# One common scale for the first weights of an attention and feed-forward kernel, and a constant scale on the sums for h

## The chip, the cores and the metric

The kernel runs on one core of a Trainium2 chip. The metric is device time in microseconds (us), the median of several runs of one program. TensorE is called PE here (PEld is its weight load), VectorE DVE, ScalarE ACT, GpSimdE POOL, and SyncE, which issues all the DMAs, SP.

## The reference

Queries are pooled in pairs, attention follows, and a feed-forward layer whose gate is a cosine:

```python
def _attn_ref(q, k, v):            # 8 batches, 8 heads, 1152 positions, 64 columns
    q_pool = q.reshape(B, H, S // 2, 2, D).mean(axis=3)
    scores = 1.0 / np.sqrt(D) * np.matmul(q_pool, k.transpose(0, 1, 3, 2))
    scores = scores - np.max(scores, axis=-1, keepdims=True)
    attn = np.exp(scores)
    attn = attn / (np.sum(attn, axis=-1, keepdims=True) + 1e-09)
    return np.matmul(attn, v)

def _moe_ref(x, w_in, w_out):      # x: 4608 x 512, w_in: 512 x 2048, w_out: 2048 x 512
    h = x @ w_in
    g = h * np.cos(h)
    return g @ w_out
```

## The kernel before

**Numbers as two halves.** The matrix products need more than one 16-bit float holds. So an operand is scaled by a power of two, rounded to a 16-bit float (the upper half), and what is left over becomes a second 16-bit float (the lower half). A product takes three matmuls: upper by upper, upper by lower, lower by upper. The bound that fixes the power of two is a maximum over the operand.

**Attention.** Two heads make a pair; there are 32 pairs, and each is worked in 10 units (`NU`), nine of them over one block of 128 keys and one (the remainder) for the last 64 queries. A unit's scores go to the one PSUM buffer `st` (L1123; the remainder L1146). ACT reads it with the exponential into `e` or `pp` (L1173). In the first pairs (`NF32`) this stays a 32-bit float and goes as it is into the product with V (L1199, remainder L1248); in later ones ACT casts the upper half (L1179) and POOL or DVE subtracts it for the lower (L1185, L1181). Ahead of a pair, PE works out its scores in tiles `m` (L757, `m0` with its number) and DVE takes their maximum (L771); the maximum is written as a column of the queries' lower half (L983) and so subtracted by the matmul. V's scaling is L1026.

**The first weights.** `w_in` and `w_out` arrive as 64-bit floats, each in 8 pieces of 128 x 1024 numbers. `weight_decode` turns a piece into 32-bit floats with three DVE steps (L516, L519, L522). For the first weights ACT then squares the piece with a running sum as its bound (L529, `AF.Square` with `accum_out`); for the second ones DVE takes the largest magnitude (L533). `weight_scale` takes two pieces: PE spreads both bounds to all partitions (`spread`, L463, tile `wam`), DVE reduces them, makes powers of two in `p2w` and their inverses `wsc` (L543, L431, L439, L547, L548; for the second weights L441 and L425 stand for L431 and L439). `weight_split` scales the piece (ACT, L556), casts the upper half (ACT, L557) and subtracts in four steps for the lower (POOL, L560). `weight_steps` runs as a generator: decode, decode, scale, split, split, and so on. The decoded first pieces lie in the memory that later holds the lower half of the second weights (`w2[1]`), four at a time.

Each two pieces have a scale of their own. So a column table `r1` holds the ratio of the two pieces' scale to the largest one, and `r1a` the same for each block of tokens (L598 to L601, L1338).

**Feed-forward.** A chunk is 256 tokens. `ffn1` (L1459) makes h in PSUM (`f`, two buffers); `evac` reads each tile three times: ACT with the scale `r1` into `hsc` (L1483), ACT with `r1a` rounded to an integer (L1486), DVE the difference from it (L1487). The cosine is a sine table (L1391); DVE multiplies (L1397), ACT casts and POOL subtracts for the halves of g (L1408, L1409). `ffn2` (L1519, the last one L1542) makes the output, which DVE scales (L1563, L1552).

**The order.** The main loop records, for each of the 320 units, scores, preparation of later pairs (`JOBS`), some feed-forward work by a credit (`FRATE`), the value product and one or so step of the weights (`SRATE`: 1.0 a unit until the first weights are ready, then 0.6). The feed-forward waits for the first weights (`w1_ready`) and for the first four pairs. `arrange` then orders each engine's instructions anew: it walks through the recorded nodes with estimated costs, and an engine that is free takes the available node that was recorded earliest. What it finds is fixed with dependencies without semaphores, so on the chip each engine works strictly in that order.

Of the kernel before, what the change touches and what calls it, by code (L numbers as in the profile page):

```python
# [9 lines left out]
F32 = mybir.dt.float32  # L10
# [10 lines left out]
P = 128  # L21
# [327 lines left out]
def tile_attention_ffn(  # L349
# [52 lines left out]
    def constants():  # L402
# [5 lines left out]
            if nf < KT:  # L408
                nc.gpsimd.memset(vc[i][:, :, nf:, D : D + 1], 1.0)

    sizes = (1, NP, B + 2, B + 2, B + 2, NWP)
    small = fix.tile([P, sum(sizes)], F32, name="small")
    ends = [sum(sizes[: i + 1]) for i in range(len(sizes))]
    w1max, p2v, p2b, fsc, osb, r1 = (
        small[:, e - n : e] for n, e in zip(sizes, ends)
    )
    p2w = fix.tile([P, 2, NWP], F32, name="p2w")
    r1a = fix.tile([P, B + 2, NWP], F32, name="r1a")
    left = dram.tile([B * LQ, DM], F32, name="left")

    w1 = [fix.tile([P, HP, DFF], F16, name=f"w1_{i}") for i in range(2)]
# [40 lines left out]
    def spread(dst, mx):  # L462
        nc.tensor.matmul(  # L463
            dst,
            mx.broadcast_to([P, P]),
            ident,
            start=True,
            stop=True,
            skip_group_check=True,
        )  # L470
# [11 lines left out]
    def big_free(n=1):  # L482
        k = len(big_alive)
        return all(x < 0 or not big_alive[x][0] for x in range(k - NBIG, k - NBIG + n))

    def big_take(shape, dtype, name):
        assert big_free()
        alive = [True]
        big_alive.append(alive)
        return sb2.tile(shape, dtype, tag="big", bufs=NBIG, name=name), alive  # L490
# [6 lines left out]
    def weight_load(wi, i):  # L497
        src, rows, width, _ = WDIM[wi]
        raw, alive = big_take([P, rows, width * WORDS], w_in.dtype, "wraw")
        ld = nc.sync.dma_start(raw, src[i].rearrange("p (r w) -> p r w", r=rows))  # L500
        if len(w_loads) > WPRE:
            held(ld, "q2T")
        elif len(w_loads) == WPRE:
            held(ld, "v")
        w_loads.append(ld)
        raws.append((raw, alive))

    def weight_decode(wi, i, ft, mx):
        raw, alive = raws.pop(0)
        if not wide:  # L510
            nc.vector.tensor_copy(ft, raw.rearrange("p r w -> p (r w)"))
        else:
            rv = raw.rearrange("p r (w two) -> p (r w) two", two=2)
            lo32, hi32 = rv[:, :, 0], rv[:, :, 1]
            fu = ft.bitcast(U32)
            nc.vector.tensor_scalar(  # L516
                fu, hi32, 0x07FFFFFF, 3, ALU.bitwise_and, ALU.logical_shift_left
            )
            nc.vector.scalar_tensor_tensor(  # L519
                fu, hi32, 0xC0000000, fu, ALU.bitwise_and, ALU.bitwise_or  # L520
            )
            nc.vector.scalar_tensor_tensor(  # L522
                fu, lo32, 29, fu, ALU.logical_shift_right, ALU.bitwise_or
            )
        alive[0] = False
        _, rows, width, dst = WDIM[wi]
        scratch = dst[0][:, :, i * width : (i + 1) * width]
        if WACT[wi]:
            nc.scalar.activation(  # L529
                scratch, ft.rearrange("p (r w) -> p r w", r=rows), AF.Square, accum_out=mx  # L530
            )
        else:
            nc.vector.tensor_reduce(  # L533
                mx, ft, axis=AX.X, op=ALU.max, apply_absolute_value=True
            )
# [15 lines left out]
    def weight_split(wi, i, ft, sc):  # L551
# [6 lines left out]
        for o in range(0, rows, rows // WCUT):  # L558
            r = slice(o, o + rows // WCUT)
            nc.gpsimd.tensor_sub(lo[:, r], fv[:, r], hi[:, r])  # L560

    def weight_steps():
        stage = w2[1].rearrange("p f e -> p (f e)").bitcast(F32)
        stage = stage.rearrange("p (a w) -> p a w", w=WN)
        todo = [(wi, i) for wi in range(2) for i in range(NWP)]
        while todo:
            (wi, i), todo = todo[0], todo[2:]
            alive = [True]
            if wi == 0:
                fts = [stage[:, i % 4 + a] for a in range(2)]  # L570
            else:
                while not big_free():
                    yield
                ft, alive = big_take([P, 2, WN], F32, "wf")
                fts = [ft[:, a] for a in range(2)]
            mx = sb2.tile([P, 2], BF16, tag="wmx", bufs=1, name="wmx")
            for a in range(2):
                while len(raws) < 2 and loads:
                    while not raws and not big_free():
                        yield  # L580
                    if not big_free():
                        break
                    weight_load(*loads.pop(0))
                if wi == 0 and i + a < 2:
                    yield
                weight_decode(wi, i + a, fts[a], mx[:, a : a + 1])
                while len(raws) < 2 and loads and big_free():
                    weight_load(*loads.pop(0))
                yield
            sc = weight_scale(wi, i, fts, mx)  # L590
            yield
            for a in range(2):
                weight_split(wi, i + a, fts[a], sc[:, a : a + 1])
                yield
            alive[0] = False
            if wi == 0 and i == NWP - 2:
                w1_ready[0] = True
                nc.vector.reduce_max(w1max, p2w[:, 0, :], axis=AX.X)  # L598
                rw = sb2.tile([P, 1], F32, tag="rw", bufs=1, name="rw")
                nc.vector.reciprocal(rw, w1max)  # L600
                nc.vector.tensor_scalar(  # L601
                    r1, p2w[:, 0, :], rw, 2.0 ** (HB - 24), ALU.mult, ALU.mult
                )

    extra = []
    fill = {}
# [725 lines left out]
    def chunk_scales(idx):  # L1332
        pm = pms.pop(idx)
        t = sb2.tile([P, 1], F32, tag="fst", bufs=1, name="fst")
        nc.vector.tensor_mul(t, pm, w1max)
        nc.vector.tensor_scalar_mul(fsc[:, idx : idx + 1], t, 2.0 ** (-4 - HB) / (2.0 * math.pi))
        nc.vector.tensor_scalar_mul(osb[:, idx : idx + 1], t, 2.0 ** (-18 - HB))
        nc.vector.tensor_scalar_mul(r1a[:, idx, :], r1, fsc[:, idx : idx + 1])  # L1338

    def split_x(xp, num, den, nt, xT_out):  # L1340
        ratio = sb2.tile([P, 1], F32, tag="ratio", bufs=1, name="ratio")
# [134 lines left out]
    def evac(ck, g, fp, ps, held):  # L1476
        hsc, y = held[:2]

        def fn():
            wp = (g * GF + fp * 2) // 2  # L1480
            yj = y[:, fp * 2 : fp * 2 + 2]
            ra = r1a[:, ck.idx, wp : wp + 1]
            nc.scalar.activation(  # L1483
                hsc[:, fp * 2 : fp * 2 + 2, :], ps, AF.Copy, scale=r1[:, wp : wp + 1]
            )
            nc.scalar.activation(yj.bitcast(I32), ps, AF.Copy, scale=ra, bias=0.25)  # L1486
            nc.vector.scalar_tensor_tensor(  # L1487
                yj, ps, ra, yj.bitcast(I32), ALU.mult, ALU.subtract
            )
            if fp == GF // 2 - 1:  # L1490
                ew_group(*held, ck.gs)

        return fn
# [305 lines left out]
```

## Time and profile before

| what | value |
|---|---|
| median of 3 runs | 1530.41 us (1527.52 to 1530.5) |
| the profiled execution | 1530.05 us, of which the span of its instructions is 1528.3 us |
| granted TensorE clock, mean over the span | 0.999 |
| first matmul of h (L1459) | 186.0 us after the start |
| first scale step of the first weights, last one (L556) | 45.9 us, 104.4 us |

Times in the profile count from the first instruction. A matmul's own duration is longer than its share of PE, since matmuls overlap; the distance from one start to the next is what it costs. A row of a group of instructions gives line, engine, operation, what is written and read, shapes and count, then the busy time in us, the mean duration in ns, and the idle time of the engine ahead of them with what ended it. Line numbers are those of the kernel before; in the order of the changed kernel the same lines stand up to 20 away (L556 is L555, L557 is L556, L1173 is L1193, L757 is L777, L1199 is L1219, L1146 is L1166).

### The profile page before, as it was taken

What the parts mean: (1) busy time and instruction counts of PE and PEld (TensorE: products, weight loads), DVE (VectorE), ACT (ScalarE), POOL (GpSimd) and SP (SyncE); (2) the same over time, 40 slices, a digit from 0 to 9 for tenths busy, and PEclk for the clock granted to TensorE, in tenths of its full rate; (3) what the DMA queues carried; (4) which work ended last, traced back from release to release, by engine and by line L of the source; (5) the groups of instructions that cost most, each with busy time, mean ns of one, the idle gap of its engine ahead of it and who ended that gap; (6) DMA issues with size and microseconds to landing.
All of it is one profiled execution on the core that took longest, in us unless ns stands there. A gap on an engine that the chain in (4) does not pass through costs nothing.

```text
span 1528.3 us, 39292 instructions
## 1 busy us (share of the span) xinstructions
PE 1492.8 (98%) x16774; PEld 1030.2 (67%) x16774; DVE 1127.6 (74%) x1552; ACT 1172.5 (77%) x1473; POOL 932.3 (61%) x793
## 2 busy tenths in 40 slices
PE   5989999999999999999999999999999999999998
PEld 3767787657666676666667667666666667666665
DVE  7889887787988788977866887888787875343332
ACT  4777679887988788887967887988888787864442
POOL 4654658886676858586565676677767665522222
PEclk9999999999999999999999999999999999999999
DMA  9979633434244454335333235445443321001000
GB/s 268 269 204 197 170 85 69 116 78 112 66 107 101 103 97 97 98 84 125 63 85 73 70 80 118 85 96 111 80 112 90 80 56 31 17 19 32 19 18 21
DMA packets 226047, 145.15 MB, mean 95 GB/s; under 512 B 202384, under 2 KB 204688, under 8 KB 223824
## 3 DMA queue, kind: packets, MB, share of 16 engines
q1 hardware_dynamic: 225872, 142.65, 40.2%
q8 instruction: 131, 2.15, 0.6%
q14 instruction: 44, 0.36, 0.1%
HBM read 74.45 MB, written 10.49 MB: 56 GB/s over the span
## 4 chain that ended last, share of the span: by engine, by line
PE 88%; DVE 6%; ACT 3%; DMA 2%; issue 1%; SPq 0%; POOL 0%; DVEq 0%; ACTq 0%; POOLq 0%
PE f L1459 20%; PE f L1519 20%; PE st L1123 14%; PE ava L1199 9%; PE avb L1199 7%; PE m L757 6%; PE st L1146 2%; PE mx L1519 1%; DVE q1s L706 1%; PE st L1459 1%; DMA kld<-in_k_dram 1%; PE mx L800 1%; PE mx L779 1%; DVE mxs L771 1%; PE avb L1459 1%
## 5 line engine op out<-in xcount | busy, mean ns | idle before, releaser
L1185 POOL TENSOR_TENSOR pp<-e,pp 128x512 f16<-128x512 f32 x374 | 461.8, 1256 | 257.0 <-ACT pp L1179 117.0
L771 DVE TENSOR_REDUCE mxs<-m 128x2 f32<-128x1024 f32 x244 | 297.6, 1220 | 104.0 <-PE m L757 102.6
L1459 PEld LDWEIGHTS <-w 128*128 128x128 f16 x3456 | 331.7, 98 | 59.6 <-issue 1.6
L1459 PE MATMUL f<-xT,w 128*128 128x256 f16 x3048 | 365.8, 273 | 0.0
L1173 ACT ACTIVATE e<-st 128x1024 f32<-128x1024 f32 x267 | 272.5, 1021 | 106.8 <-PE st L1123 84.8
L1519 PE MATMUL f<-w,g 128*128 128x512 f16 x1440 | 332.9, 379 | 0.7 <-DVE y L1487 0.7
L1409 POOL TENSOR_TENSOR g<-hsc,g 128x512 f16<-128x512 f32 x144 | 192.8, 1360 | 162.7 <-ACT g L1408 160.9
L1179 ACT CAST pp<-e 128x1024 f16<-128x1024 f32 x267 | 278.9, 1044 | 10.3 <-PE ava L1199 2.5
L1199 PEld LDWEIGHTS <-pp 128*128 128x128 f16 (+1 forms) x7062 | 240.3, 100 | 62.3 <-issue 14.6
L1519 PEld LDWEIGHTS <-g 128*128 128x128 f16 x1680 | 158.5, 98 | 177.2 <-DVE y L1487 0.9
L1199 PE MATMUL ava<-vc,pp 128*128 128x65 f16 (+5 forms) x4646 | 236.7, 200 | 1.0 <-DVE lx L1313 1.0
L1123 PE MATMUL st<-q1T,k 128*128 128x512 f16 x576 | 219.0, 380 | 4.5 <-ACT pp L1173 4.4
L1123 PE MATMUL st<-q2T,k 128*128 128x512 f16 x576 | 218.8, 380 | 0.0
L1199 PE MATMUL avb<-vc,pp 128*128 128x65 f16 (+1 forms) x3196 | 198.3, 200 | 0.0
L1123 PEld LDWEIGHTS <-k 128*128 128x128 f16 x1152 | 105.3, 99 | 100.0 <-issue 10.8
L1397 DVE TENSOR_TENSOR hsc<-hsc,y 128x512 f32<-128x512 f32 x144 | 135.1, 978 | 26.0 <-ACT y L1391 25.8
L757 PE MATMUL m<-k,q1T 128*128 128x512 f16 x496 | 147.0, 379 | 4.2 <-DVE mxs L771 2.3
L1483 ACT ACTIVATE hsc<-f,small 128x512 f32<-128x512 f32 x127 | 86.6, 682 | 83.9 <-PE f L1459 83.7
L1487 DVE SCALAR_TENSOR_TENSOR y<-f,r1a,y 128x512 f32<-128x512 f32 x127 | 94.6, 745 | 61.1 <-ACT y L1486 56.3
L1181 DVE TENSOR_TENSOR pp<-e,pp 128x1024 f16<-128x1024 f32 x80 | 125.6, 1570 | 17.7 <-ACT pp L1179 17.5
L1408 ACT CAST g<-hsc 128x512 f16<-128x512 f32 x144 | 83.3, 613 | 11.6 <-PE f L1519 11.6
L1486 ACT ACTIVATE y<-f,r1a 128x512 int32<-128x512 f32 x127 | 86.2, 679 | 0.0
(180 smaller groups left out, 1786.2 us busy)
## 6 DMA issues: line engine op xcount, KB each, us to landing
vld<-in_v_dram SPq DMA_DIRECT2D x32, 576.0 KB, 3.9
kld<-in_k_dram SPq DMA_DIRECT2D x30, 576.0 KB, 4.2
qld<-in_q_dram SPq DMA_DIRECT2D x30, 576.0 KB, 4.4
k<-k SPq DMA_DIRECT2D x31, 288.0 KB, 3.6
wraw<-in_moe_w_in_dram SPq DMA_DIRECT2D x8, 1024.0 KB, 9.0
wraw<-in_moe_w_out_dram SPq DMA_DIRECT2D x8, 1024.0 KB, 5.9
out_dram<-ob SPq DMA_DIRECT2D x32, 256.0 KB, 2.4
left<-lx SPq DMA_DIRECT2D x64, 16.0 KB, 2.0
```

The costliest lines, as they stand in the source:

```text
L757: nc.tensor.matmul(banks[h], q1T[n][:, h * QT + t, :], kmain(n, k1[n % 3], c, h), start=True, stop=True, skip_group_check=True,),
L771: nc.vector.reduce_max(mxs[n][:, t : t + QT + 1 : QT, c], m, axis=AX.X)
L1123: nc.tensor.matmul(s[:, y, :].rearrange("p (t c) -> p t c", c=P), kcol(p, w, j, h), x[:, h * QT : (h + 1) * QT, :], start=part == 0, stop= ...
L1173: nc.scalar.activation(e, s, AF.Exp, scale=exp_scale, bias=l_add)
L1179: nc.scalar.copy(pp[:, 0, c0:n], e[:, c0:n])
L1181: nc.vector.tensor_sub(pp[:, 1, c0:n], e[:, c0:n], pp[:, 0, c0:n])
L1185: nc.gpsimd.tensor_sub(pp[:, 1, c], e[:, c], pp[:, 0, c])
L1199: mm = nc.tensor.matmul(out, w, x, start=start, stop=False, skip_group_check=True)
L1397: nc.vector.tensor_mul(hj, hj, y[:, j : j + 2])
L1409: nc.gpsimd.tensor_sub(gt[:, 1], hj, gt[:, 0])
L1459: mm = nc.tensor.matmul(ps[:, fi, :], w1[wt][:, hp, fs], ck.xT[hp][:, xi, cs], start=n == 0, stop=n == 3 * HP - 1, skip_group_check=True,)
L1519: nc.tensor.matmul(po, gt[:, gi, f % 2, ts_], w2[wt][:, f, :], start=f == 0 and (gi, wt) == (0, 0), stop=f == NF - 1 and (gi, wt) == (1, 0),)
```

## The change

A new generator `first_weights` takes the place of `weight_steps` for the first weights. It decodes all eight pieces, four into `w2[1]` and four into `w2[0]`, each with its square sum into one column of a tile `mx`; reduces the eight to one, spreads it with one matmul, and makes one bound `w1max` and one inverse `sc`; then splits all eight pieces with `sc`. `weight_steps` goes on with the second weights as before. The tables `r1` and `r1a` go: h leaves PSUM with the constant 2^(HB - 24), and the two other reads take the block's column `fsc`.

```diff
+    def first_weights():
+        stage = [
+            w.rearrange("p f e -> p (f e)").bitcast(F32).rearrange("p (a w) -> p a w", w=WN)
+            for w in (w2[1], w2[0])
+        ]
+        fts = [stage[i // 4][:, i % 4] for i in range(NWP)]
+        mx = sb2.tile([P, NWP], BF16, tag="wmx1", bufs=1, name="wmx1")
+        for i in range(NWP):
...
+            weight_decode(0, i, fts[i], mx[:, i : i + 1])
...
+            yield
+        one = sb2.tile([P, 1], BF16, tag="wmx2", bufs=1, name="wmx2")
+        nc.vector.reduce_max(one, mx, axis=AX.X)
+        am = psum.tile([P, P], F32, tag="f", bufs=2, name="wam")
+        spread(am, one)
+        mw = sb2.tile([P, 1], F32, tag="rw", bufs=1, name="rw")
+        nc.vector.reduce_max(mw, am, axis=AX.X)
+        all_max_end(w1max, mw, WACT[0])
+        sc = sb2.tile([P, 1], F32, tag="wsc1", bufs=1, name="wsc1")
+        nc.vector.reciprocal(sc, w1max)
+        nc.vector.tensor_scalar_mul(sc, sc, 2.0**14)
+        yield
+        for i in range(NWP):
+            weight_split(0, i, fts[i], sc)
+            yield
+        w1_ready[0] = True
+
     def weight_steps():
...
-        todo = [(wi, i) for wi in range(2) for i in range(NWP)]
+        yield from first_weights()
+        todo = [(1, i) for i in range(NWP)]
...
-            if wi == 0 and i == NWP - 2:
-                w1_ready[0] = True
-                nc.vector.reduce_max(w1max, p2w[:, 0, :], axis=AX.X)
-                rw = sb2.tile([P, 1], F32, tag="rw", bufs=1, name="rw")
-                nc.vector.reciprocal(rw, w1max)
-                nc.vector.tensor_scalar(
-                    r1, p2w[:, 0, :], rw, 2.0 ** (HB - 24), ALU.mult, ALU.mult
-                )
...
-        nc.vector.tensor_scalar_mul(fsc[:, idx : idx + 1], t, 2.0 ** (-4 - HB) / (2.0 * math.pi))
+        nc.vector.tensor_scalar_mul(fsc[:, idx : idx + 1], t, 2.0**-28 / (2.0 * math.pi))
...
-        nc.vector.tensor_scalar_mul(r1a[:, idx, :], r1, fsc[:, idx : idx + 1])
...
-            ra = r1a[:, ck.idx, wp : wp + 1]
+            ra = fsc[:, ck.idx : ck.idx + 1]
             nc.scalar.activation(
-                hsc[:, fp * 2 : fp * 2 + 2, :], ps, AF.Copy, scale=r1[:, wp : wp + 1]
+                hsc[:, fp * 2 : fp * 2 + 2, :], ps, AF.Copy, scale=2.0 ** (HB - 24)
             )
```

More of the change, by code (lines that the diff above doesn't have):

```diff
@@ L409, in constants @@
                 nc.gpsimd.memset(vc[i][:, :, nf:, D : D + 1], 1.0)
-    sizes = (1, NP, B + 2, B + 2, B + 2, NWP)
+    sizes = (1, NP, B + 2, B + 2, B + 2)
     small = fix.tile([P, sum(sizes)], F32, name="small")
     ends = [sum(sizes[: i + 1]) for i in range(len(sizes))]
-    w1max, p2v, p2b, fsc, osb, r1 = (
+    w1max, p2v, p2b, fsc, osb = (
         small[:, e - n : e] for n, e in zip(sizes, ends)
@@ L417, in tile_attention_ffn @@
     p2w = fix.tile([P, 2, NWP], F32, name="p2w")
-    r1a = fix.tile([P, B + 2, NWP], F32, name="r1a")
     left = dram.tile([B * LQ, DM], F32, name="left")
@@ L560, in weight_split @@
             nc.gpsimd.tensor_sub(lo[:, r], fv[:, r], hi[:, r])
+    def first_weights():
[6 more added lines that the diff above has]
+        for i in range(NWP):
+            while len(raws) < 2 and loads:
+                while not raws and not big_free():
+                    yield
+                if not big_free():
+                    break
+                weight_load(*loads.pop(0))
+            if i < 2:
+                yield
+            weight_decode(0, i, fts[i], mx[:, i : i + 1])
+            while len(raws) < 2 and loads and big_free():
+                weight_load(*loads.pop(0))
+            yield
[9 more added lines that the diff above has]
+        nc.vector.tensor_scalar_mul(sc, sc, 2.0**14)
+        yield
+        for i in range(NWP):
+            weight_split(0, i, fts[i], sc)
+            yield
+        w1_ready[0] = True
@@ L562, in weight_steps @@
     def weight_steps():
-        stage = w2[1].rearrange("p f e -> p (f e)").bitcast(F32)
-        stage = stage.rearrange("p (a w) -> p a w", w=WN)
-        todo = [(wi, i) for wi in range(2) for i in range(NWP)]
+        yield from first_weights()
+        todo = [(1, i) for i in range(NWP)]
         while todo:
             (wi, i), todo = todo[0], todo[2:]
[L568 to L575, printed above, removed]
+            while not big_free():
+                yield
+            ft, alive = big_take([P, 2, WN], F32, "wf")
+            fts = [ft[:, a] for a in range(2)]
@@ L583, in weight_steps @@
                     weight_load(*loads.pop(0))
-                if wi == 0 and i + a < 2:
-                    yield
                 weight_decode(wi, i + a, fts[a], mx[:, a : a + 1])
@@ L1479, in fn @@
         def fn():
-            wp = (g * GF + fp * 2) // 2
             yj = y[:, fp * 2 : fp * 2 + 2]
-            ra = r1a[:, ck.idx, wp : wp + 1]
+            ra = fsc[:, ck.idx : ck.idx + 1]
             nc.scalar.activation(
-                hsc[:, fp * 2 : fp * 2 + 2, :], ps, AF.Copy, scale=r1[:, wp : wp + 1]
+                hsc[:, fp * 2 : fp * 2 + 2, :], ps, AF.Copy, scale=2.0 ** (HB - 24)
             )
```

## The prediction

> **What bounds the kernel now.** I read the page first: engine shares, then the chain.
>
> ```profile
> span 1528.3 us, 39292 instructions
> PE 1492.8 (98%) x16774; PEld 1030.2 (67%) x16774; DVE 1127.6 (74%) x1552; ACT 1172.5 (77%) x1473; POOL 932.3 (61%) x793
> PE 88%; DVE 6%; ACT 3%; DMA 2%; issue 1%; SPq 0%; POOL 0%; DVEq 0%; ACTq 0%; POOLq 0%
> ```
>
> TensorE is busy in 98% of the span and makes 88% of the chain. Its work hardly changes here, so the question is how much TensorE stands still, before and after. Second view: busy times by stretch (start:end, length, then busy time and count of PE, PEld, DVE, ACT, POOL, the granted clock, DMA).
>
> ```profile
> 40.00:90.00 50.00, 47.66 (x466) 37.59 (x465) 45.07 (x72) 40.49 (x52) 29.15 (x27) 1.00 1.05 271
> 90.00:110.00 20.00, 16.29 (x169) 11.99 (x168) 18.72 (x29) 15.19 (x21) 10.93 (x14) 1.00 0.69 207
> 110.00:165.00 55.00, 53.78 (x487) 43.17 (x487) 50.51 (x80) 36.73 (x50) 28.96 (x30) 1.00 0.81 187
> 165.00:180.00 15.00, 12.98 (x135) 8.71 (x134) 11.47 (x20) 10.26 (x14) 8.87 (x9) 0.89 0.54 140
> 200.00:1528.00 1328.00, 1317.72 (x15143) 896.41 (x15142) 953.74 (x1293) 1037.00 (x1294) 823.78 (x673) 1.00 0.34 77
> ```
>
> PE stands still for 2.3, 3.7, 1.2 and 2.0 us in the first four stretches, and for 10.3 us in the 1328 us after 200. All the first-weight work lies before 110 us, in attention alone, where DVE is busy for 18.7 of 20 us. Idle time there can't be caught up later, since nothing later has slack on PE: each microsecond won or lost counts once in the total.
>
> What stops PE there I read in ACT's row of instructions (third view, the timeline: start, duration, operation, in brackets the idle time before it). L1173 is the exponential of one attention unit. The scores have one PSUM buffer (`st`), so PE can't write the next unit's scores until this one's exponential is done.
>
> ```profile
> 82.79 1.02 ACT L1173 ACTIVATE pp<-st 128x1024 f32<-128x1024 f32 x1 [1.55 <-PE st L1123]
> 83.71 1.14 ACT L556 ACTIVATE w<-w,wsc 128x1024 f32<-128x1024 f32 x1
> 84.75 0.23 ACT L983 ACTIVATE qs<-m 128x9 f16<-128x9 f32 x1
> 84.88 1.05 ACT L557 CAST w<-w 128x1024 f16<-128x1024 f32 x1
> 85.83 1.25 ACT L1026 ACTIVATE vc<-vld,sv 128x1152 f32<-128x1152 f32 x1
> 86.99 1.13 ACT L556 ACTIVATE w<-w,wsc 128x1024 f32<-128x1024 f32 x1
> 88.03 1.00 ACT L1173 ACTIVATE pp<-st 128x1024 f32<-128x1024 f32 x1
> ...
> 98.96 1.04 ACT L529 ACTIVATE w<-w 128x1024 f16<-128x1024 f32 x1
> 99.91 0.19 ACT L529 ACTIVATION_READ_ACCUMULATOR w<-w 128x1 bf16 x1
> ...
> 100.19 1.00 ACT L1173 ACTIVATE pp<-st 128x1024 f32<-128x1024 f32 x1
> ...
> 102.27 1.15 ACT L556 ACTIVATE w<-w,wsc 128x1024 f32<-128x1024 f32 x1 [0.91 <-DVE wsc L548]
> 103.45 1.04 ACT L557 CAST w<-w 128x1024 f16<-128x1024 f32 x1
> 104.40 1.15 ACT L556 ACTIVATE w<-w,wsc 128x1024 f32<-128x1024 f32 x1
> ...
> 107.01 1.02 ACT L1173 ACTIVATE pp<-st 128x1024 f32<-128x1024 f32 x1
> ```
>
> Weight work between two exponentials parts them by 5.2 us (82.79 to 88.03) and by 6.8 us (100.19 to 107.01). The first lies in a stretch where PE hardly stops, the second in the one that loses 3.7 us. So other work for PE covers a parting of some 5 us; beyond that PE waits.
>
> **The change part by part.** *The hole in the exponentials.* The scale of any piece is now known only after all eight, so all sixteen ACT steps of the splits (scale, L556, now L555; cast, L557, now L556) come free at once, and the planner takes what was recorded earlier. This is ACT's row, first before (around the third pair of pieces; `w` is the weight, `pp<-st` the exponential), then now.
>
> ```order
> L1173 ACTIVATE pp<-st 128x1024 x2
> L556 ACTIVATE w_1_84<-w_1_84,wsc 128x1024
> L983 ACTIVATE qs_71<-m 128x9
> L557 CAST w_0_81<-w_1_84 128x4x256
> L1026 ACTIVATE vc_75<-vld,sv 128x18x64
> L556 ACTIVATE w_1_84<-w_1_84,wsc 128x1024
> L1173 ACTIVATE pp<-st 128x1024
> L557 CAST w_0_81<-w_1_84 128x4x256
> L1173 ACTIVATE pp<-st 128x1024 x2
> ```
>
> ```order
> L555 ACTIVATE w_1_83<-w_1_83,wsc_742 128x1024
> L556 CAST w_0_80<-w_1_83 128x4x256
> L555 ACTIVATE w_1_83<-w_1_83,wsc_742 128x1024
> L1003 ACTIVATE qs_71<-m 128x9
> L555 ACTIVATE w_1_83<-w_1_83,wsc_742 128x1024 x2
> L556 CAST w_0_80<-w_1_83 128x4x256
> L555 ACTIVATE w_0_82<-w_0_82,wsc_742 128x1024
> L1046 ACTIVATE vc_75<-vld,sv 128x18x64
> L555 ACTIVATE w_0_82<-w_0_82,wsc_742 128x1024
> L556 CAST w_0_80<-w_1_83 128x4x256
> L555 ACTIVATE w_0_82<-w_0_82,wsc_742 128x1024 x2
> L1193 ACTIVATE pp<-st 128x1024
> ```
>
> Two scale steps at most stood between exponentials; now eight, three casts, the maximum's write (L1003) and a V scaling (L1046) stand in one row, with an exponential ahead and one behind. Their price, start to start in the rows above: a scale step followed by its own cast 1.18 (102.27 to 103.45), the seven others 1.04 each (86.99 to 88.03), casts 0.95 each (103.45 to 104.40), L1003 0.13, L1046 1.16: 1.18 + 7.28 + 2.85 + 0.13 + 1.16 = 12.6 us. The first waits for the scale: from the last piece's square to the first scale step 98.96 to 102.27 = 3.3 us. So from the square to the end of the next exponential pass 3.3 + 12.6 + 1.0 = 16.9 us, 16.8 of them after the previous exponential. What PE has meanwhile stands in its row (around unit 19; `m0` the score tiles for the maxima, `st_1007` the scores that wait for that exponential):
>
> ```order
> L1219 MATMUL avb_817<-vc_1_76,pp_980 128x65 x4
> ...
> L777 MATMUL m0_933<-k1_0_91,q1T_798 128x512
> ...
> L777 MATMUL m0_962<-k1_0_91,q1T_798 128x512
> ...
> L777 MATMUL m0_987<-k1_0_91,q1T_798 128x512
> ...
> L777 MATMUL m0_1040<-k1_0_91,q1T_798 128x512
> L1166 LDWEIGHTS k1_2_93
> L1166 MATMUL st_1007<-q1T_393,k1_2_93 128x64
> ```
>
> ```order
> L757 MATMUL m0_943<-k1_0_92,q1T_803 128x512
> L1199 MATMUL ava_768<-vc_1_76,pp_991 128x65 x4
> L1199 MATMUL avb_822<-vc_1_76,pp_991 128x65 x4
> ...
> L757 MATMUL m0_972<-k1_0_92,q1T_803 128x512
> ...
> L1146 MATMUL st_1018<-q1T_394,k1_2_94 128x64
> ```
>
> The upper row is now, the lower before: one `m0` tile stood between the last attention-value work and the next scores; now four do. They fill part of the hole. Prices from PE's timeline:
>
> ```profile
> 84.43 0.59 PE L757 MATMUL m<-k,q1T 128*128 128x512 f16 x2
> 84.86 0.38 PE L1123 MATMUL st<-q1T,k 128*128 128x512 f16 x1
> ...
> 85.72 1.00 PE L1199 MATMUL avb<-vc,pp 128*128 128x65 f32 x8
> 86.56 1.06 PE L1199 MATMUL ava<-vc,pp 128*128 128x65 f32 x8
> ```
>
> Start to start: an `m0` tile 0.43, a unit's scores 0.86, a group of four value matmuls 0.84. From the scores before the hole to `st_1007` PE has two scores (1.72), six `m0` tiles (2.58), five value groups (4.2) and small ones, which I put at 0.35: 8.85 us in 16.8. **PE idles about 8.0 us.** The bounds: 16.8 if PE had no work there; 5 if PE enters 3 us behind ACT, about one unit.
>
> *The clock.* The row 165:180 has a granted clock of 0.89. By pieces (columns as above):
>
> ```profile
> 172.00:174.00 2.00, 2.00 (x17) 1.72 (x16) 1.97 (x3) 0.00 (x0) 0.26 (x1) 0.81 0.25 52
> 174.00:176.00 2.00, 2.00 (x14) 1.06 (x14) 1.27 (x6) 0.53 (x1) 0.00 (x0) 0.50 1.11 171
> 176.00:178.00 2.00, 2.00 (x24) 0.88 (x21) 1.12 (x1) 1.97 (x3) 0.35 (x1) 0.83 0.72 188
> ```
>
> After a stretch in which PE idled 2 us in all, its clock fell to half: 2 x (0.19 + 0.50 + 0.17) = 1.7 us of work lost. The hole is emptier, so I add 1.7 (0 to 3.4). The Trainium skill ("TensorE: Matmul & The Clock Gate", section "HAM oscillation") sets the danger at idle gaps over about 3.4 us. By that rule the `m0` tiles, which cut the hole into shorter gaps, would keep the clock up and the sum would be 1.7 lower. The trace disagrees: no gap in these rows was that long, and the clock fell, so the row decides.
>
> *Stalls that go.* The partings of before that cost 3.7 us in 90:110 lose their weight work. The hole's leftovers (five casts, a K cast) still stand among the exponentials behind it, so I credit half, -1.9 (0 to -3.7).
>
> *DVE.* The scale group per pair of pieces is one group for all. Its rows, from DVE's groups between 40 and 106 us:
>
> ```profile
> L771 DVE TENSOR_REDUCE mxs<-m 128x2 f32<-128x1024 f32 x18 | 21.9, 1219 | 3.5 <-PE m L757 3.4
> ...
> L543 DVE TENSOR_REDUCE wmw<-wam 128x2 f32<-128x256 f32 x4 | 1.7, 417 | 0.3 <-PE wam L463 0.3
> ...
> L431 DVE TENSOR_SCALAR wmw<-wmw 128x2 uint32<-128x2 uint32 x4 | 1.1, 282 | 0.1
> ...
> L439 DVE TENSOR_SCALAR p2w<-wmw 128x2 f32<-128x2 f32 x4 | 0.7, 170 | 0.1
> L548 DVE TENSOR_SCALAR wsc<-wsc 128x2 f32<-128x2 f32 x4 | 0.7, 169 | 0.1
> L547 DVE RECIPROCAL wsc<-p2w 128x2 f32<-128x2 f32 x4 | 0.7, 166 | 0.2
> ```
>
> 417 + 282 + 170 + 169 + 166 = 1.2 us; three groups fewer is 3.6 us of DVE. PE's idle time before the hole is only the 2.3 of 40:90, so I take -1 (0 to -3.6). Seven broadcast matmuls of 128 columns fewer (`wam`), at the `m0` tile's 0.43 for 1024 columns, are 0.05 each, -0.4.
>
> *The reads of h.* ACT's copy of the sum gets a constant for a column, and the column table r1a goes.
>
> ```profile
> L1483 ACT ACTIVATE hsc<-f,small 128x512 f32<-128x512 f32 x127 | 86.6, 682 | 83.9 <-PE f L1459 83.7
> ...
> L1173 ACT ACTIVATE pps<-f 128x128 f32<-128x128 f32 x3 | 0.8, 271 | 0.0
> ...
> L1338 DVE TENSOR_SCALAR r1a<-small 128x8 f32<-128x8 f32 x10 | 4.6, 464 | 0.0
> ...
> PE f L1519 <- DVE y L1487: 0.7, 2, 0.4
> ```
>
> Exponentials, with constant scale and bias, take 271 ns for 128 columns and 1.02 us for 1024; between them 512 columns cost 0.59, so each copy may save 0.09 us, 13 us of ACT over 144. ACT is 77% busy, and of PE's waits the last row is all that its list lays to these reads: 0.7 us (waiter, releaser, sum, times, longest). I count 0, and +-3 for the new order over the 1328 us with their 10.3 us of PE idle.
>
> *Sum.* +8.0 + 1.7 - 1.9 - 1 - 0.4 = +6.4 us. The profiled execution took 1530.05 us (span 1528.3), 0.4 below the median of 1530.41, so 1530.05 + 6.4 = **1536.4 us**. A measurement of this kernel can tell about 0.2%, 3 us.
>
> **The rivals.** *DVE sets the pace and the hole is free: no change.* In the new order DVE has, between the scale and the reduction that follows `st_1007`, six `m0` reductions of 1.22 us and 3.5 us of other steps, 10.8 of 13.6 us. If DVE is the bound of this stage, the hole costs 13.6 - 10.8 = 2.8 and the clock 1.7, against 3.6 + 0.4 + some stalls: 1530 us. For it: DVE's 18.7 of 20 us in 90:110. Against: over 110:165 DVE works 50.5 of 55 us and PE 53.8, so PE is the tighter one. It decides where the four `m0` tiles leave PE no stall in units 20 to 24. Chance 0.23.
>
> *Faster: the lighter reads count.* If ACT's 13 us and DVE's 4.6 us of r1a halve PE's 10.3 us after 200, 5 us go, and with the hole free as above: 1525 us. Against it is the 0.7 us in the list of waits. It needs both, so 0.14.
>
> *The hole is heavier.* No stall goes, the clock falls twice (3.4), and the lower halves on POOL, eight pieces in one row now, hold back what attention needs by half the hole again: 8.0 + 3.4 + 4 = 15.4, 1545 us. For it: POOL's subtractions can no longer be spread. Against: POOL is busy for 10.9 of 20 us. Chance 0.13. The forecast keeps 0.50.
>
> **How the numbers follow.** The forecast's own range is 1533.5 to 1541. Slower takes forecast and heavier hole, 0.63; within 0.2% 0.23; faster 0.14. For 8 in 10 the range goes from 1527, leaving out the faster end, to 1545.
>
> **What would show it.** Right: in the changed profile two exponentials near 85 to 105 us are 14 to 16 us apart with a row of L555 between, PE idles about 8 us there in pieces ended by `m` reductions and an exponential, and a half clock follows; after 200 us PE's idle time stays near 10 us; the copy of h falls from 682 towards 590 ns with no effect. Wrong: the exponentials stay under 8 us apart, or PE's idle time before 200 us is not larger than before, or the difference arises after 200 us.

## The result, and the profile after

| what | before | after |
|---|---|---|
| median | 1530.41 us (5 runs, 1527.52 to 1531.61) | 1537.04 us (5 runs, 1536.22 to 1543.44) |
| ratio | | 1.0059, 95% interval 1.0044 to 1.0074 |
| the profiled execution | 1530.05 us, span 1528.3 | 1543.44 us, span 1541.7 |

The change costs 6.6 us, 0.6%, against a forecast of +6.4. The profiled execution of after is the slowest of its five, 6.4 us above their median, so its rows show where time goes and only roughly how much. Totals and chain of after:

```profile
span 1541.7 us, 39270 instructions
PE 1499.8 (97%) x16767; PEld 1032.2 (67%) x16767; DVE 1101.1 (71%) x1525; ACT 1162.1 (75%) x1473; POOL 913.4 (59%) x793
PE 85%; DVE 4%; ACT 4%; DMA 3%; issue 2%; SPq 0%; POOL 0%; ACTq 0%; DVEq 0%; POOLq 0%
```

DVE works 26.5 us less and ACT 10.4 us less than before (1127.6 and 1172.5), and the kernel is slower: neither sets the end. PE's busy time grew by 7 us although it has seven matmuls fewer, since a matmul at half clock counts as busy for longer (a pair of matmuls on `m` 1.01 us instead of 0.59, in the rows of the first place below). By stretches (start:end, length, busy time and count of PE, PEld, DVE, ACT, POOL, the granted clock, DMA):

```profile
40.00:90.00 50.00, 48.57 (x469) 37.65 (x468) 43.07 (x63) 32.59 (x46) 9.25 (x8) 1.00 0.94 262
90.00:110.00 20.00, 14.51 (x92) 9.98 (x92) 13.71 (x18) 16.78 (x20) 17.14 (x21) 0.66 0.77 241
165.00:200.00 35.00, 29.11 (x283) 21.13 (x281) 28.56 (x43) 22.10 (x28) 20.81 (x23) 0.85 0.54 119
200.00:1300.00 1100.00, 1094.08 (x13344) 744.49 (x13342) 857.34 (x1173) 909.46 (x1129) 742.07 (x614) 1.00 0.40 90
```

In 90:110 PE starts 92 matmuls where it started 169, is idle for 5.5 us, and runs at a clock of 0.66. In 165:200 it is idle for 5.9 us. From 200 to 1300 PE is busy for 1094.1 us, before for 1093.4: the loss is not there. The same row of before for the third stretch:

```profile
165.00:200.00 35.00, 32.98 (x346) 24.85 (x345) 31.29 (x41) 24.46 (x31) 22.08 (x23) 0.95 0.55 133
```

So there are two places, and the second, 3.9 us more idle time at 165 to 200 us, stands nowhere in the prediction.

**The first place.** ACT's row of after (start, duration, operation, in brackets the idle time before it):

```profile
84.87 1.05 ACT L528 ACTIVATE w<-w 128x1024 f16<-128x1024 f32 x1
85.81 0.20 ACT L528 ACTIVATION_READ_ACCUMULATOR w<-w 128x1 bf16 x1
86.54 1.02 ACT L1193 ACTIVATE pp<-st 128x1024 f32<-128x1024 f32 x1 [0.53 <-PE wam L462]
87.63 1.15 ACT L555 ACTIVATE w<-w,wsc 128x1024 f32<-128x1024 f32 x1
...
98.10 2.19 ACT L555 ACTIVATE w<-w,wsc 128x1024 f32<-128x1024 f32 x2
100.19 1.00 ACT L1193 ACTIVATE pp<-st 128x1024 f32<-128x1024 f32 x1
```

The two exponentials are 13.65 us apart, and the row of splits between them takes 12.56 us (87.63 to 100.19). PE's row of the same time:

```profile
85.42 0.38 PE L1143 MATMUL st<-q1T,k 128*128 128x512 f16 x1
...
88.72 0.38 PE L1143 MATMUL st<-q1T,k 128*128 128x512 f16 x1
...
94.50 0.59 PE L777 MATMUL m<-k,q1T 128*128 128x512 f16 x2 [1.32 <-DVE mxs L791]
96.41 0.92 PE L777 MATMUL m<-k,q1T 128*128 128x512 f16 x2 [1.32 <-DVE mxs L791]
...
98.65 1.01 PE L777 MATMUL m<-k,q1T 128*128 128x512 f16 x2 [1.10 <-DVE mxs L791]
101.24 0.21 PE L1166 MATMUL st<-q1T,k 128*128 128x64 f16 x1 [1.58 <-ACT pp L1193]
```

As forecast, three gaps are ended by reductions of `m` and the fourth by the exponential. The `m` tiles of 96.41 and 98.65 last longer than the one of 94.50 (0.92 and 1.01 against 0.59): the clock has fallen. By pieces (columns as above):

```profile
94.00:96.00 2.00, 0.59 (x2) 0.19 (x2) 1.32 (x2) 2.00 (x3) 1.90 (x4) 1.00 0.84 157
96.00:98.00 2.00, 1.13 (x6) 0.55 (x6) 1.83 (x3) 2.00 (x3) 2.00 (x3) 0.64 0.36 37
101.00:106.00 5.00, 4.76 (x46) 4.39 (x45) 4.09 (x6) 3.35 (x5) 4.85 (x6) 0.50 0.67 259
106.00:110.00 4.00, 3.83 (x12) 1.95 (x13) 1.32 (x5) 2.43 (x4) 2.96 (x5) 0.50 0.85 322
```

The half clock stays until 110 us, for 9 us after PE has all its work again.

**The second place.** ACT's rows of after, and behind them PE's:

```profile
174.13 1.15 ACT L707 CAST kst<-kld 128x1152 f16<-128x1152 f32 x1 [1.40 <-issue]
175.19 1.02 ACT L1193 ACTIVATE e<-st 128x1024 f32<-128x1024 f32 x1
```

```profile
172.78 0.38 PE L1143 MATMUL st<-q1T,k 128*128 128x512 f16 x1 [0.96 <-ACT pp L1193]
176.26 0.59 PE L1143 MATMUL st<-q1T,k 128*128 128x512 f16 x1 [2.34 <-ACT e L1193]
...
181.03 1.01 PE L777 MATMUL m<-k,q1T 128*128 128x512 f16 x2 [1.32 <-DVE mxs L791]
```

PE waits for exponentials that ACT does late, and has little else: the cast of K (L707), ahead of which ACT stood idle for 1.40 us, comes before the exponential in ACT's row. The clock falls here too in this execution (0.85 in 165:200, and the pair of matmuls on `m` at 181.03 lasts 1.01 us).

To see where the order gives PE how much, I laid PE's matmuls in the trace against the order one by one, cut them into attention units (from a unit's first score matmul to the next unit's), and took each unit's work as its matmuls at the median start-to-start distance of their line and shape. What a unit lasts beyond its work I call its excess. Units 41, 42 and 43 hold 3.3, 2.9 and 3.1 us of work before, and 1.3, 1.0 and 7.0 us after: the value work and a score tile that kept PE busy between exponentials now stand behind the scores of unit 43.

The excess in us, by ranges of units, from one profile each (the runs from e1_spread on are told below; e4_warm and e10_ahead_warm count their idle matmuls as work):

```
run              0-17  18-23  24-39  40-45  46-99  100-318   sum   profiled us
before            3.3    4.5   -0.5    3.9   -1.2     0.9   10.9     1530.05
after             4.7   11.0   -0.6    9.4   -1.6     2.2   25.0     1543.44
e1_spread         3.2    3.6    1.2    6.7   -2.0     2.5   15.2     1531.78
e2_reads          3.1    5.0   -0.6    2.8   -2.1    -0.5    7.8     1527.76
e3_weights        2.8   10.7   -0.7    6.3   -1.4     1.7   19.4     1535.64
e4_warm           2.8    2.5   -0.7    7.4   -2.0     2.4   12.2     1533.88
e5_delay          3.8    2.6   -0.2    2.0    5.2    -0.9   12.4     1529.89
e6_delay_alone    3.6    8.4    6.2    0.9    5.2    -0.5   23.8     1541.46
e7_ahead          4.3    7.4   -0.4    1.4   -0.9     2.2   14.0     1532.92
e8_both           4.6    1.4   -0.1    2.0    5.2    -0.5   12.7     1530.03
e9_six            3.8    1.4    0.4    3.2    6.1     3.5   18.4     1533.69
e10_ahead_warm    6.3    0.5    0.2    2.2    4.6     1.3   15.1     1538.11
e11_columns       4.2    1.4    0.0    2.9    0.7     0.5    9.8     1528.28
e12_shift         2.6    4.4    0.7    2.3    1.9     1.2   13.0     1530.78
```

A line's time less its sum lies between 1515.3 and 1520.0 us, but for the two with idle matmuls (1521.7 and 1523.0). What the sum leaves out thus differs by up to 4.7 us from run to run, so the table is used for places, and times are compared by medians. Of after's 9.4 us in units 40 to 45 some belong to the half clock of its execution: the profile of e3_weights, the same first weights, has a full clock there and 6.3 us.

### The profile page after: what moved, and what is told of

Same layout as the page of the kernel before. It is cut to its first block, busy times and chain, and to the rows that moved or that the text cites. A ratio compares the mean times of both kernels' runs of the same rounds, so it can differ in the third digit from the quotient of the medians.

```text
span 1541.7 us, 39270 instructions
## 1 busy us (share of the span) xinstructions
PE 1499.8 (97%) x16767; PEld 1032.2 (67%) x16767; DVE 1101.1 (71%) x1525; ACT 1162.1 (75%) x1473; POOL 913.4 (59%) x793
## 4 chain that ended last, share of the span: by engine, by line
PE 85%; DVE 4%; ACT 4%; DMA 3%; issue 2%; SPq 0%; POOL 0%; ACTq 0%; DVEq 0%; POOLq 0%
PE f L1478 19%; PE f L1537 19%; PE st L1143 14%; PE ava L1219 9%; PE avb L1219 7%; PE m L777 6%; PE st L1166 2%; PE mx L1537 1%; DMA vld<-in_v_dram 1%; DVE mxs L791 1%; DMA wraw<-in_moe_w_in_dram 1%; PE mx L799 1%; PE mx L820 1%; PE st L1478 1%; ACT e L1193 1%
## 5 line engine op out<-in xcount | busy, mean ns | idle before, releaser
L777 PE MATMUL m<-k,q1T 128*128 128x512 f16 x496 | 150.4, 387 | 9.9 <-DVE mxs L791 7.8
L1505 DVE SCALAR_TENSOR_TENSOR y<-f,small,y 128x512 f32<-128x512 f32 x127 | 94.6, 746 | 73.0 <-ACT y L1504 72.6
L1501 ACT ACTIVATE hsc<-f 128x512 f32<-128x512 f32 x127 | 75.1, 592 | 91.0 <-PE f L1478 91.0
L708 POOL TENSOR_TENSOR kst<-kld,kst 128x1152 f16<-128x1152 f32 x30 | 72.8, 2428 | 33.2 <-ACT kst L707 33.0
```

The source lines that it names most:

```text
L777: nc.tensor.matmul(banks[h], q1T[n][:, h * QT + t, :], kmain(n, k1[n % 3], c, h), start=True, stop=True, skip_group_check=True,),
```

## The experiments

Theory at the start: the eight splits in one row make the hole, and the hole with its half clock is the whole loss. Rivals: the loss is in the second place or after it, or in the reads.

**e1_spread: the row taken apart.** The changed kernel, with the scale step of piece n kept behind the exponential of unit 18 + n by an added dependency for the planner.

```diff
+SPREAD0 = 18
...
-        nc.scalar.activation(ft, ft, AF.Copy, scale=sc)
+        first = nc.scalar.activation(ft, ft, AF.Copy, scale=sc)
+        if wi == 0:
+            w1_scales.append(first)
...
+    for n, x in enumerate(w1_scales):
+        after(x, exps[SPREAD0 + n])
     arrange(tc, nc, extra, fill)
```

> The changed kernel, with one thing added: in the planner the scale step of piece n may not stand ahead of the exponential of unit 18 + n, so that one scale step and one cast at most stand between two exponentials. Nothing of the computation changes. Theory (the row of eight scale steps makes a hole of 13.65 us between two exponentials, PE idles in it and then runs at half clock): the longest parting of exponentials between 80 and 130 us falls under 7 us, the half clock near 100 us goes, and the median falls by 5 to 9 us, to 1528 to 1532. Rival (the 6.6 us come from elsewhere, from the new order of the later stages or from the later start of the feed-forward): 1535 or more.

Measured: 1534.05 us (6 runs, 1531.78 to 1535.31), ratio to before 1.0032 (1.0019 to 1.0045). Its stretches (columns as above):

```profile
90.00:110.00 20.00, 16.98 (x174) 12.70 (x173) 18.86 (x23) 16.08 (x21) 14.93 (x18) 1.00 0.79 219
165.00:200.00 35.00, 29.52 (x308) 21.93 (x308) 30.58 (x48) 22.96 (x30) 23.00 (x21) 1.00 0.41 106
```

The hole and its half clock are gone (174 matmuls and clock 1.00 in 90:110, better than before's 16.29 us), but only 3 of the 6.6 us went with them, which is between the theory's range and the rival's. (The longest parting of exponentials is 7.21 us, 89.16 to 96.37, where under 7 was expected; ACT itself is idle for 3.15 us of it.) The second row is poor here too (PE busy for 29.52 us, before for 32.98), without any half clock: the second place doesn't follow from the hole. The theory of one place fell. The 3 us aren't the hole's whole price either: by the table 7.4 us go in units 18 to 23, and 1.8 come back in units 24 to 39.

**e2_reads: the constant reads alone.** The kernel before, with the change's constant scale for h and the block's column for the other two reads; the ratio of the pieces' scales is left out.

```diff
...
-            ra = r1a[:, ck.idx, wp : wp + 1]
+            ra = fsc[:, ck.idx : ck.idx + 1]
             nc.scalar.activation(
-                hsc[:, fp * 2 : fp * 2 + 2, :], ps, AF.Copy, scale=r1[:, wp : wp + 1]
+                hsc[:, fp * 2 : fp * 2 + 2, :], ps, AF.Copy, scale=2.0 ** (HB - 24)
             )
```

> The kernel before with the second part of the change alone: h leaves PSUM with the constant scale and the two other reads take the block's column; the first weights keep a scale for each two pieces. The ratio of a piece's scale to the largest one is left out. Theory (this part costs nothing and gains nothing, since ACT is not what PE waits for): 1527 to 1533.5, the same as before within 3 us, although the copy of h falls from 682 to about 590 ns. Rival (the reads are where the loss or a gain lies): outside of that.

Measured: 1526.75 us (12 runs, 1525.08 to 1528.66), 0.9984 (0.9975 to 0.9994): 2.5 us faster than before in the same session (1529.26), 0.25 us under the expected range and so on the rival's side, and the fastest kernel of the study. **e3_weights** is the counterpart: the new first weights, with column reads (the table filled for eight equal scales).

> The changed kernel with the first part alone: one common scale for the first weights as changed, but h leaves PSUM with a column table as before (the table now holds the same constant eight times). Theory: the hole is as in the changed kernel, 1535 to 1540, with the copy of h at 682 ns. Rival (the loss lies in the constant reads, or in both together): below 1533.

Measured: 1537.17 us (6 runs, 1535.64 to 1540.2), 1.0055 (1.0042 to 1.0069). The copy of h, first in after, then in e3_weights (groups of ACT: busy time, mean ns of one, idle time before):

```profile
L1501 ACT ACTIVATE hsc<-f 128x512 f32<-128x512 f32 x127 | 75.1, 592 | 91.0 <-PE f L1478 91.0
```

```profile
L1507 ACT ACTIVATE hsc<-f,small 128x512 f32<-128x512 f32 x127 | 86.6, 682 | 75.2 <-PE f L1483 75.1
```

The constant saves 90 ns a copy, ACT then waits longer for PE, and the two kernels differ by 0.13 us. The loss belongs to the first weights and the order that comes with them, not to the reads. What the reads had gained in the kernel before wasn't explained yet.

**e4_warm: the half clock by itself.** The changed kernel, with 90 idle matmuls of 128 columns for PE in the hole, whose results nothing reads.

```diff
+WARM = (91.7, 90, 0.1)
...
+        for n in range(WARM[1]):
+            mm = nc.tensor.matmul(
+                big_am[:, P : 2 * P], ident, ident, start=True, stop=True, skip_group_check=True
+            )
+            fill[mm.ins.name] = WARM[0] + WARM[2] * n
```

> The changed kernel with 90 idle matmuls of 128 columns on PE inside the hole, 5 us of PE work that nothing reads, between the m tiles. The hole itself stays. Theory (of the 6.6 us the hole's idle time is the larger part, and the half clock after it, 13.65 us long in the profiled execution, adds 3 to 5 us): the clock stays full between 90 and 115 us and the median falls by 2 to 5 us, to 1532 to 1535. Rival (the half clock costs nothing, since the exponentials set the pace there anyway): no change, 1536 to 1540, though the clock is full. A second rival (the matmuls delay what PE has to do): over 1540.

Measured: 1533.69 us (9 runs, 1532.01 to 1534.78), 1.0031 (1.0021 to 1.0041), 3.35 us under after, inside the expected range. The clock stays full (columns as above):

```profile
90.00:110.00 20.00, 17.60 (x230) 13.87 (x229) 18.23 (x22) 17.29 (x21) 18.33 (x18) 1.00 0.73 228
```

PE's rows: the scores ahead of the hole, those that end it, and the first scores of unit 24, in e4_warm and then, for the last, in after.

```profile
86.10 0.38 PE L1150 MATMUL st<-q1T,k 128*128 128x512 f16 x1
...
98.62 0.19 PE L1173 MATMUL st<-q1T,k 128*128 128x64 f16 x1 [0.58 <-ACT pp L1200]
...
109.61 0.38 PE L1150 MATMUL st<-q1T,k 128*128 128x512 f16 x1
```

```profile
115.65 0.38 PE L1143 MATMUL st<-q1T,k 128*128 128x512 f16 x1
```

The hole is the same length: 86.10 to 98.62 is 12.52 us, and 88.72 to 101.24 in after is 12.52 too. Behind it PE needs 10.99 us to unit 24 with the idle matmuls and 14.41 us without. So the half clock costs nothing in the hole and 3.4 us behind it.

**e5_delay and e6_delay_alone: the second place.** The planner takes steps in the order in which the units record them, one weight step a unit. The old first weights had 22 such steps (2 and 4 times 5), the new ones have 19 (2 + 8 + 1 + 8), so every step of the second weights is recorded three units earlier, at another point of the attention pairs' rhythm. e6_delay_alone adds three empty steps to the changed kernel, e5_delay to e1_spread:

```diff
+        for _ in range(3):
+            yield
         w1_ready[0] = True
```

> The changed kernel with the scale steps spread as in the first experiment (1534.05 us there), and with three empty steps added at the end of the first weights, so that the steps of the second weights are recorded in the same units as before the change (the change leaves 19 steps where there were 22, so they came three units earlier). The planner then puts the last 128 columns of that pair's scores, and the bound of m after it, back into units 41 and 42, where only about 1.0 to 1.3 us of PE work a unit was left. Theory (the rest of the loss is this second place, PE's excess over its work in units 40 to 46 being 6.7 us against 3.9 before): 1530.5 us, 1528.5 to 1532, and that excess 3 to 4.5 us. Rival (the rest comes from elsewhere, such as longer work on DVE or the smaller stalls at 110 to 140 us): it stays at 1533 to 1535 us whatever the excess in those units does.

Measured: 1531.49 us (12 runs, 1529.6 to 1534.81), 1.0015 (1.0006 to 1.0024), 2.6 us under e1_spread, with an excess in units 40 to 45 of 2.0 us, less than the 3 to 4.5 expected. Its row of the second place:

```profile
165.00:200.00 35.00, 33.46 (x370) 26.35 (x368) 31.82 (x47) 24.22 (x31) 23.79 (x22) 1.00 0.58 133
```

PE starts 370 matmuls where e1_spread started 308. The theory of the second place holds. But in units 46 to 99 the excess is 5.2 us, where the kernels so far have -1.2 to -2.1: the new order had a stall of its own there, so the 2.6 us are what is left after it.

> The changed kernel with the three empty steps alone; the scale steps stay in one row, so the hole near 100 us and its half clock stay. Theory of two separate places: 1533 us, 1531.5 to 1535, with PE's excess in units 18 to 24 still 10 to 11 us and in units 40 to 46 3 to 4.5 us. Rival (the second place only follows from the hole, as lateness handed on): the empty steps alone change nothing and it stays at 1536 to 1538 us.

Measured: 1541.46 us (5 runs, 1538.68 to 1543.6), 1.0079 (1.0066 to 1.0092). Both expectations missed. The hole stayed (excess 8.4 in units 18 to 23), the second place closed (0.9), and a third opened, in units 33 and 34. POOL's, DVE's and PE's rows there:

```profile
137.85 2.40 POOL L710 TENSOR_TENSOR kst<-kld,kst 128x1152 f16<-128x1152 f32 x1
```

```profile
138.06 3.26 DVE L521 SCALAR_TENSOR_TENSOR wf<-wraw,wf 128x1024 uint32<-128x1024 uint32 x1
141.25 1.21 DVE L793 TENSOR_REDUCE mxs<-m 128x2 f32<-128x1024 f32 x1
```

```profile
142.51 0.59 PE L779 MATMUL m<-k,q1T 128*128 128x512 f16 x2 [1.94 <-DVE mxs L793]
```

A decode step of DVE, 1.22 us in the median of its group, took 3.26 us beside a subtraction on POOL; the reduction behind it came late; PE stood still for 1.94 us, and the clock fell:

```profile
143.00:148.00 5.00, 5.00 (x29) 4.16 (x28) 3.71 (x7) 0.29 (x1) 0.74 (x2) 0.56 0.85 203
148.00:154.00 6.00, 6.00 (x25) 4.17 (x25) 1.31 (x3) 1.02 (x1) 0.00 (x0) 0.51 0.78 218
```

**e7_ahead: a smaller dose of the hole.** The three empty steps ahead of the eight splits instead of behind them, in the changed kernel.

> The changed kernel with the three empty steps ahead of the eight splits instead of behind them. The second weights come as in the experiment before; and of the eight scale steps five instead of eight stand between the same two exponentials. Theory (the hole's price goes with the number of scale steps in one row, about 1.15 us for each): the two exponentials are 9.5 to 10.5 us apart instead of 13.65, PE's excess in units 18 to 24 falls to 6 to 8 us from 11, and the time is 1531 us, 1528.5 to 1533. Rival (the hole has one price as long as some steps stand in one row, since the half clock comes all the same): 1533 to 1535 us, as with the empty steps behind the splits.

Measured: 1531.51 us (11 runs, 1529.31 to 1534.28), 1.0012 (1.0004 to 1.0021). ACT's row:

```profile
85.69 1.02 ACT L1195 ACTIVATE pp<-st 128x1024 f32<-128x1024 f32 x1 [0.53 <-PE wam L462]
...
95.17 1.00 ACT L1195 ACTIVATE pp<-st 128x1024 f32<-128x1024 f32 x1
```

Five scale steps instead of eight, and two casts instead of three, part the exponentials by 9.48 us, the excess in units 18 to 23 falls from 11.0 to 7.4 us and that in 40 to 45 to 1.4. As the theory had it; the half clock still lasts 10.24 us.

**e8_both, e9_six and e10_ahead_warm: a way out?** e8_both has e1_spread's dependencies and the empty steps ahead of the splits.

> The changed kernel with the scale steps spread over the units and the three empty steps put ahead of the splits: no hole, and the second weights recorded where they were before the change. It differs from the spread kernel with the empty steps behind the splits (1531.49 us) only in what is recorded when in units 13 to 24. Theory (what is left over the reads alone, 1526.75 us, is small stalls that each new order places anew, not the cost of the first weights' work): 1526 to 1531 us, and PE's excess over its work spread otherwise than in that kernel (2.0 us in units 40 to 46, 5.1 in 46 to 100). Rival (the first weights cost some 4 to 5 us more than before in whatever order): 1531 to 1533 us with the hole and the second place both closed.

Measured: 1529.75 us (12 runs, 1526.54 to 1531.88), 1.0001 (0.9991 to 1.0010). With both places closed the loss is gone. Its first place:

```profile
90.00:110.00 20.00, 18.27 (x189) 14.20 (x188) 18.18 (x22) 16.70 (x22) 15.75 (x20) 1.00 0.79 212
```

PE is busy for 2 us more than before in this stretch; the table has 5.2 us of excess in units 46 to 99 against it.

e9_six has six empty steps ahead of the splits and no added dependency.

> The changed kernel with six empty steps ahead of the eight splits and no other rule. Two scale steps instead of five (three empty steps, 1531.51 us) or eight (none, 1537.04 us) then stand between the same two exponentials, and three ahead of the next. Theory (the hole's price goes with the number of steps in one row): partings of the exponentials of 6 to 8 us, PE's excess in units 18 to 24 down to 3 to 5 us from 7.4, no half clock there, 1528 us, 1526 to 1531. Rival (second weights recorded three units later than before the change open a stall of their own elsewhere): excess in units 18 to 24 falls all the same, and the time stays at 1531 us or above.

Measured: 1534.43 us (8 runs, 1533.37 to 1535.57), 1.0029 (1.0016 to 1.0042). The hole closed, further than expected (partings of 5.4 and 5.2 us, excess 1.4, no half clock there), but the rival's number came true: with the second weights three units later than before, 6.1 us of excess stand in units 46 to 99 and 3.5 us behind.

e10_ahead_warm is e7_ahead with e4_warm's idle matmuls.

> The kernel with three empty steps ahead of the splits (1531.51 us), with 90 idle matmuls of 128 columns for PE in and behind the hole; they add work that nothing reads. Theory (in the hole the half clock is paid apart from the idle time: 10.24 us at half clock there, of which the idle matmuls in the changed kernel gave back 3.3 us): no half clock between 85 and 112 us, 1528.5 us, 1527 to 1530.5. Rival (the half clock lies beside waiting and costs next to nothing once only five scale steps stand in the row): 1531 to 1532.5 us.

Measured: 1536.31 us (6 runs, 1533.9 to 1538.11), 1.0040 (1.0027 to 1.0054); both missed. The half clock near the hole went, but the idle matmuls gave the planner another order, with 6.3 us of excess in units 0 to 17 and 4.6 in 46 to 99. It tells nothing of the half clock's price; e4_warm does.

**e11_columns and e12_shift: the reads again, and the order by itself.** e11_columns is e8_both with column reads; e12_shift is e2_reads with three empty steps at the end of the first weights.

> The kernel with the steps spread and the empty steps ahead of the splits (1529.75 us), but h and y read their scale from columns of a table again, filled for eight equal scales. Together with the reads alone (1526.75 us against 1529.26) it tells what the constant reads are worth. Theory A (the lighter reads are worth some 2.5 us wherever the order leaves PE waiting for ACT and DVE): 1532 us, 1531 to 1534. Theory B (the reads are worth nothing, as the changed kernel with column reads, 1537.17 us beside 1537.04, says; what the reads alone gained came with the order they brought): 1529 to 1530.5 us.

Measured: 1528.52 us (11 runs, 1527.44 to 1531.15), 0.9997 (0.9989 to 1.0006). A little under theory B's range. Column reads are no slower than constant ones (1529.75): the reads are worth nothing, as in e3_weights beside after.

> The kernel before with the constant reads alone (1526.75 us; the ratio of the pieces' scales is left out there and here) and with three empty steps at the end of the first weights, so that nothing but the order of what comes after changes. Theory (a new order alone places new stalls of 2 to 6 us, as six empty steps and the idle matmuls showed): outside 1525.5 to 1528 us, and as the gaps were tuned for the old order rather slower, 1528 to 1533. Rival (an order moved by three units costs nothing by itself): 1525.5 to 1528 us.

Measured: 1534.59 us (10 runs, 1530.26 to 1536.56), 1.0032 (1.0020 to 1.0044), 7.8 us above e2_reads and 1.6 above the theory's own range: a new order cost more than the stalls of 2 to 6 us that it allowed for. No work was added; only the order differs. Its profile shows 3 us of them at most, since the profiled run is the second fastest, 1530.78 us. Part of the rest goes with the clock: the two runs with a mean of 1.000 took 1530.26 and 1530.78 us, the three at 0.996 and 0.997 took 1535.35 to 1536.56. Not all does, as one at 0.999 took 1535.91.

## Why the prediction was right, and where it was not

The time and its sign were right, with 1537.04 for 1536.4 us, and so was the main mechanism, the hole and the clock behind it. That the sum came so close was partly luck: its terms for the first place are 1.3 us too high by the table, the gains of 1.4 us in front of it can't be told, and the second place is missing.

- *The hole, +8.0.* Right in place, cause and form, and too large by 1.3 us: the excess of unit 19 is 6.7 us (12.5 us long, 5.8 of work), and the idle pieces in brackets, of which the forecast expected about 8 us, add up to 5.3. The parting of 13.65 us is a little under the 14 to 16 forecast. The row of splits was 12.56 us for 12.6. What was mis-sized is the wait for the scale, 3.3 us from the start of the last square; it took 2.8 (84.87 to 87.63), and an exponential was done in it. So from the scores before the hole to those behind it 15.8 us passed (85.42 to 101.24), not 16.8.
- *The clock, +1.7.* Right to add, and sized at half: e4_warm shows 3.4 us, the upper bound. The forecast took one lapse of 3.41 us at 173 us for the pattern; from inside the hole on the half clock lasted 13.65 us.
- *The rule on idle gaps.* The Trainium skill ("TensorE: Matmul & The Clock Gate", section "HAM oscillation") sets the danger at gaps over about 3.4 us. Here the clock fell between 96 and 98 us, behind two brackets of 1.32 us, and the longest bracket of the whole hole is 1.58 us. That page's section "A second HAM failure mode: psum-queue depth-cycling" says that frequent short idle times let the clock go back and forth too; this trace agrees with that sentence in so far as short gaps came before the fall, and e4_warm, where the gaps were filled, kept a clock of 1.00.
- *Stalls that go, -1.9.* Half was credited, and nearly all went: of the 11.0 us of excess in units 18 to 23, 6.7 are the hole and 3.4 the clock, which leaves 0.9 of the 4.5 us of before. So this place cost 11.0 - 4.5 = 6.5 us, where the terms gave 8.0 + 1.7 - 1.9 = 7.8.
- *DVE, -1, and the broadcasts, -0.4.* DVE's time fell, but no gain can be told: in units 0 to 17 the excess is 3.3 us before and between 2.8 and 4.7 in the kernels with the new decoding (6.3 in e10_ahead_warm). The first weights' work doesn't all end before 110 us, as the prediction says; POOL's last subtraction for them starts at 112.1.
- *The reads, 0.* Right: e3_weights beside after and e11_columns beside e8_both show no gain, though a copy fell from 682 to 592 ns as forecast.
- *The failing step: a new order after the hole, "+-3 for the new order over the 1328 us".* It was looked for only after 200 us. The steps of the second weights moved three units, which the difference in the number of steps gives away, and opened the second place, between 165 and 200 us: 9.4 us of excess in after's profile, 6.3 in e3_weights', 3.9 before. Closing it (e5_delay against e1_spread) brought 2.6 us.

The rivals: DVE didn't set the pace. Three gaps of PE in the hole are ended by its reductions, but DVE is idle ahead of each of the three itself, waiting for PE's `m` tile, and it is the exponential that ends the hole. DVE's rows of after:

```profile
93.22 1.23 DVE L791 TENSOR_REDUCE mxs<-m 128x2 f32<-128x1024 f32 x1 [0.94 <-PE m L777]
95.13 1.23 DVE L791 TENSOR_REDUCE mxs<-m 128x2 f32<-128x1024 f32 x1 [0.68 <-PE m L777]
...
97.37 1.23 DVE L791 TENSOR_REDUCE mxs<-m 128x2 f32<-128x1024 f32 x1 [0.17 <-PE m L777]
```

The lighter reads don't count. The heavier hole was half right: the clock cost the 3.4 us that it gave, but no gap of PE in the hole is ended by POOL.

Closed: the two places, by e1_spread, e4_warm, e5_delay, e7_ahead and e8_both; with both mended the kernel runs as before. That last time alone would prove little, since e12_shift and e2_reads differ by 7.8 us through the order alone; what ties the loss to the two places is that the excess falls in the units where each edit acts. Left open: why e2_reads is 2.5 us faster than before. Its reads are worth nothing in two other orders and its order is another, so I take it for the order, but no run shows which stall went. The stalls of 5 to 6 us in units 46 to 99 of e5_delay, e6_delay_alone, e8_both and e9_six weren't followed either.

## What to carry to other kernels

When a value becomes known later, all that waited for it comes free at once, and a planner that takes what was recorded first sends it off in one row, ahead of what the bottleneck waits for: spread it, or record it later. A change in the number of steps moves everything recorded behind it; compare the bottleneck's work between waits there too, not only where the edit is. And in a kernel 98% full, orders that do the same work differ by 8 us (1526.75 and 1534.59), so a gain under 0.5% is judged only with the order held fixed or tried in several versions.

## What was not expected of the hardware

- Inside the spans, TensorE's half clock came in pieces of 3.41, 6.83, 10.24 and 13.65 us in these traces, one to four times 3.413, and lasted on while PE was busy for 4.76 of 5 us. The Trainium skill ("TensorE: Matmul & The Clock Gate", section "What's actually happening") gives a free-running window of 3413 ns; the lengths agree. Its table has the full clock come back after at least one busy window; after the hole PE was busy for 9 us, two to three windows, before it did.
- A stall can thus be paid twice: 1.94 us of idle time in e6_delay_alone was followed by 10.24 us at half clock, and in after the half clock behind the hole cost 3.4 us, as e4_warm shows.
- DVE's decode of 1.22 us took 3.26 us when POOL's subtraction had begun 0.21 us ahead of it. The subtraction ended at 140.25, and 140.25 + 1.22 = 141.47 is near DVE's end at 141.32. The Trainium skill ("SBUF — State Buffer", section "Who interferes with whom") has a DVE instruction with two SBUF inputs, as the decode is, contend with a POOL instruction that reads SBUF, and the order of issue decide who is blocked; the row agrees.
